# Moving the Gram parts of the fifth step and the first two output transposes to earlier places in a planned order

## The chip, the cores and the metric

The kernel runs on one core of a Trainium2 chip. The metric is device time of one execution in microseconds (us). A profile of one further execution gives, for each engine, when every instruction started and how long it took. Engines: PE is the matrix engine (TensorE; its weight loads are listed apart as PEld), DVE the vector engine, ACT the scalar engine, POOL is GpSimd, SP only issues transfers. Each engine works through its own instructions strictly in the order of the program; where one has to wait, everything behind it on that engine waits too.

## The reference, cut to what matters

Three stages follow each other. The first is a linear attention with a delta rule, token after token (4 batches, 8 heads, 768 tokens, 48 columns per head):

```python
for t in range(S):
    kt, vt, bt = (k_n[:, :, t], v[:, :, t], beta[:, :, t, None])
    y[:, :, t] = np.einsum('bhd,bhde->bhe', q[:, :, t], state)
    v_old = np.einsum('bhde,bhd->bhe', state, kt)
    state = state + bt[:, :, :, None] * np.einsum('bhd,bhe->bhde', kt, vt - v_old)
```

The second is a product layer on the 3072 rows of y: `a = x @ w1; b = x @ w2; h = a * b @ w3; x = h @ w_out` (384 columns, 1024 inside). The third is a soft mixture of experts: `logits = x @ phi`, a softmax over all tokens that makes 32 slot inputs, two layers per expert, a softmax over the slots that spreads the results back.

## The kernel before, in words

**Attention in chunks.** The 768 tokens are cut into 24 steps of 32 tokens; all 4 batches and 8 heads of a step are worked on together. Two steps make a pair (12 pairs, the tiles `kl` of keys and queries are loaded per pair, the names kl_112 to kl_115 are the first four pairs), four steps make a group (6 groups). For each step, small matmuls make its Gram parts (`g_step`, L474 on: keys times keys and keys times queries, into PSUM banks gp). Their evacuation (`g_evac`, L432 on) has three pieces: DVE masks the key part into the tile dg (L437), ACT copies a part to the buffer `praw` (L448) and four blocks to kl (L472), and POOL multiplies praw by a mask into kl (L457 or L464). From dg, a group's four steps together, DVE solves the small triangular systems (`solve_steps`; the transpose L519 starts it, then some 20 us of short dependent DVE operations, L607 ends it). A step's chain (`chain_steps`) then runs: POOL scales v (`pre`, L660), PE takes the old values (ks, L674) which DVE subtracts (L676), PE applies the solve (vp, L685), ACT copies the result into sv (L649), PE makes the outputs (yp, L695; ACT copies them to ys, L698) and, once in a pair, the new state (sacc, L705; ACT copies it to sv, L649). The last part of a step's chain, `xt`, turns the outputs ys by three PE transposes (xp, L717), which ACT rounds (L720) and DVE subtracts (L721) into the tile xT that the product layer reads.

**Product layer.** For each pair 8 products `ab` (18 matmuls each, L770) with w1 and w2; ACT and DVE multiply the halves (L774, L779). w3, w_out and phi are folded into one 1024x32 matrix, wphi.

**Weights.** All of w1, w2, w3 and w_out arrive as 64-bit floats and are converted on the chip (`to_f32`, L325 to L342): five operations, DVE L333, ACT L334, DVE L335, L337 and L339, then a product L342 on POOL (or DVE). w1 and w2 come first (tiles gx, raw_w and t_w; results wsl, with a rounding rest `lo` made by PE L358 and L359 and copied by ACT L360). Then w_out and w3 in 32 pieces of the tile `hold`: 8 of wo, then 24 of w3, each with PE transposes (wot L386, w3tw L407), an ACT copy (woT L388, w3T L409) and a PE product (wm L391, w3tw L411).

**What sets the order.** Every piece of work is put into a list with a number, its place (`when`, `spread`); the list is sorted by it, and the pieces are recorded in that order, which gives each instruction its priority. A planner then goes through the program with a model of the engines and lets each engine take the ready instruction of the highest priority, so that a piece with an earlier place can also move others. Numbers below zero are work ahead of the first product. `G1` is the place of the Gram parts of pair 2 (the fifth and sixth step, tile kl_114), `G2` that of pair 3 (kl_115); the second group's solve, solve 1 (dg, gl_1441, w_1535), needs both. PSUM buffers are handed out in recorded order too: the Gram parts of the second group use the two banks of `ab`, where a bank's next user waits until the last one is evacuated. The buffers of praw have the tag ys, of which there are two, shared with the outputs ys and with the solve's t. SP issues nearly all transfers in one queue; a reload of a kl tile waits there until the pair before is done with it.

## Time and profile before

| | |
|---|---|
| median of 3 runs | 621.5 us (618.1 to 623.37) |
| the profiled execution's own time | 618.01 us |
| its span in the profile | 616.2 us |
| PE busy | 566.3 us (92%) |
| DVE busy | 392.6 us (64%) |
| ACT busy | 282.4 us (46%) |
| POOL busy | 126.1 us (20%) |
| mean granted clock of PE | 0.933 |

Times within the profile count from the start of the span. A granted clock of 1.00 is 2.4 GHz and 0.50 is 1.2 GHz; a stretch with a number between had both. The first 98 us hold the first group's solve, the conversion of w1 and w2 and the chains of the first steps; solve 1 runs from 98 to 121 us; from there on products, chains and solves run side by side, with the conversion of wo and w3 up to about 215 us. The experts fill the last 60 us.

### The profile page before, as it was taken

To read this page: it belongs to the slowest core of one execution; us is meant where nothing else is said; L and a number is where in the kernel's file an instruction comes from. 1 tells how busy PE (TensorE), PEld (TensorE's weight loads), DVE (VectorE), ACT (ScalarE), POOL (GpSimd) and SP (SyncE) were. 2 spreads that over 40 slices of the span, in tenths; PEclk is the share of its full clock that TensorE was granted. 3 is DMA by queue.
4 is the path that set the end of the run, shared out by engine and by line. 5 is a ranking of instruction groups with operands and counts; after the bars stand their busy time and mean duration, and the time that the engine had idled before them with its cause. 6 is when DMAs were issued, how large, how long until landed. Compare 5 with 4: busy or idle time off the path is not lost.

```text
span 616.2 us, 26161 instructions
## 1 busy us (share of the span) xinstructions
PE 566.3 (92%) x11506; PEld 460.1 (75%) x11508; DVE 392.6 (64%) x1275; ACT 282.4 (46%) x709; POOL 126.1 (20%) x191
## 2 busy tenths in 40 slices
PE   4888769797989999999989999999999999999996
PEld 3455558696777878879879897988988888885364
DVE  6997786977699549832499827987981313224124
ACT  1147674455466454654535545435444354323023
POOL 0111185253464260122200103013111000000100
PEclk7678866989698999999999999999999999999997
DMA  5934881048547732401304040312425133689818
GB/s 121 287 98 149 221 223 55 3 137 254 168 131 214 202 82 68 100 17 28 90 3 101 16 101 16 111 53 80 139 87 196 53 110 99 229 274 319 333 63 278
DMA packets 36945, 81.73 MB, mean 133 GB/s; under 512 B 4352, under 2 KB 17792, under 8 KB 35584
## 3 DMA queue, kind: packets, MB, share of 16 engines
q1 hardware_dynamic: 36544, 79.54, 43.2%
q8 instruction: 90, 1.47, 1.0%
q10 hardware_dynamic: 288, 0.52, 0.4%
q14 instruction: 23, 0.19, 0.1%
HBM read 69.57 MB, written 10.49 MB: 130 GB/s over the span
## 4 chain that ended last, share of the span: by engine, by line
PE 48%; DVE 35%; POOL 5%; ACT 4%; DMA 3%; issue 3%; SPq 1%; DVEq 0%; POOLq 0%; ACTq 0%
PE ab L770 19%; DVE xl L581 6%; DVE tmp L578 6%; PE gp L492 2%; PE vp L685 2%; PE sacc L1215 2%; DVE gl L519 2%; PE gp L787 2%; PE hp L1194 2%; PE ks L674 2%; DMA hold<-wo 2%; DVE xl L556 2%; PE w3tw L407 2%; DVE gT L779 2%; PE yp L695 2%
## 5 line engine op out<-in xcount | busy, mean ns | idle before, releaser
L770 PE MATMUL ab<-xT,wsl 128*128 128x256 f32 x1728 | 243.3, 293 | 0.3 <-DVE gT L779 0.2
L770 PEld LDWEIGHTS ab<-xT,wsl 128*128 128x128 f32 x1728 | 218.6, 194 | 11.3 <-issue 5.7
L779 DVE TENSOR_TENSOR gT<-ab,bs 128x256 f32<-128x256 f32 x84 | 35.0, 420 | 85.1 <-ACT bs L774 84.4
L774 ACT COPY bs<-ab 128x256 f32<-128x256 f32 x96 | 35.6, 372 | 79.7 <-PE ab L770 76.2
L660 POOL TENSOR_TENSOR v<-v,nnT 128x384 f32<-128x384 f32 x24 | 21.0, 873 | 193.0 <-DMA v<-vt 86.7
L581 DVE TENSOR_TENSOR xl<-xl,tmp 128x84 f32<-128x84 f32 (+35 forms) x220 | 51.1, 263 | 0.8
L649 ACT COPY sv<-vp 32x384 f32<-32x384 f32 x96 | 45.2, 471 | 11.7 <-PE vp L685 10.0
L578 DVE TENSOR_TENSOR tmp<-xl 128x84 f32<-128x84 f32 (+35 forms) x220 | 47.5, 246 | 0.5
L492 PE MATMUL gp<-kl 48*32 48x128 f32 (+1 forms) x1152 | 37.7, 265 | 4.7 <-ACT kl L472 4.6
L342 POOL TENSOR_TENSOR hold<-hold 128x384 f32<-128x384 f32 (+1 forms) x32 | 31.7, 991 | 42.6 <-DVE hold L339 15.1
L472 ACT COPY kl<-gp 32x256 f32<-32x256 f32 x72 | 26.2, 364 | 22.6 <-DVE kl L457 21.7
L492 PEld LDWEIGHTS gp<-kl 48*32 48x32 f32 x1152 | 27.0, 115 | 12.5 <-ACT kl L472 6.1
L788 ACT COPY gtok<-gp 128x512 f32<-128x512 f32 x48 | 28.2, 588 | 16.4 <-PE gp L787 15.6
L787 PE MATMUL gp<-cs,gT 128*128 128x128 f32 x168 | 26.7, 277 | 2.1 <-DVE gT L779 1.8
L335 DVE SCALAR_TENSOR_TENSOR hold<-hold 128x384 int32<-128x384 int32 (+1 forms) x32 | 22.5, 702 | 8.0 <-ACT hold L334 7.5
L674 PE MATMUL ks<-sv,kl 48*32 48x48 f32 (+2 forms) x1344 | 24.4, 212 | 2.2 <-issue 1.6
L334 ACT ACTIVATE hold<-hold,cs 128x384 int32<-128x384 int32 (+1 forms) x32 | 18.9, 590 | 16.4 <-DVE hold L333 15.3
L685 PEld LDWEIGHTS vp<-v,w 32*32 32x32 f32 x1536 | 20.3, 110 | 7.3 <-issue 3.6
L685 PE MATMUL vp<-v,w 32*32 32x48 f32 x1536 | 25.1, 210 | 0.6 <-DVE w L634 0.6
L674 PEld LDWEIGHTS ks<-sv,kl 48*32 48x32 f32 (+2 forms) x1344 | 20.1, 113 | 6.9 <-issue 3.6
L695 PE MATMUL yp<-sv,kl 112*32 112x48 f32 (+2 forms) x1408 | 24.7, 209 | 0.4 <-issue 0.4
L695 PEld LDWEIGHTS yp<-sv,kl 112*32 112x32 f32 (+2 forms) x1408 | 19.5, 110 | 5.3 <-issue 2.6
(252 smaller groups left out, 965.5 us busy)
## 6 DMA issues: line engine op xcount, KB each, us to landing
hold<-w SPq DMA_DIRECT2D x16, 384.0 KB, 3.7
v<-vt SPq DMA_DIRECT2D x24, 192.0 KB, 2.9
kl<-kq SPq DMA_DIRECT2D x9, 512.0 KB, 7.4
kk<-kt SPq DMA_DIRECT2D x12, 384.0 KB, 6.2
kl<-w1e SPq DMA_DIRECT2D x6, 768.0 KB, 5.4
unitg<-w2e SPq DMA_DIRECT2D x6, 768.0 KB, 4.7
kl<-kq SPq DMA_DIRECT2D x9, 384.0 KB, 5.0
gx<-w SPq DMA_DIRECT2D x4, 768.0 KB, 5.2
```

What stands on the lines that cost most here:

```text
L342: last_m.append(E.tensor_tensor(out=w, in0=m, in1=w, op=ALU.mult))
L492: m = T.matmul(gp[trow(n, b), h - hs[0]], lhsT=t[r, k[j], kc], rhs=t[r, slots, kc], start=True, stop=True)
L578: V.tensor_tensor(out=tmp[:, 0:n, lo:hi], in0=x[:, j + 1:32, j:j + 1].to_broadcast([128, n, hi - lo]), in1=x[:, j:j + 1, lo:hi].to_broadca ...
L581: V.tensor_tensor(out=x[:, j + 1:32, lo:hi], in0=x[:, j + 1:32, lo:hi], in1=tmp[:, 0:n, lo:hi], op=ALU.add)
L649: A.copy(o, i)
L674: T.matmul(kp[o, h], lhsT=kl[r, (5, 1)[b // 2] if t2 else 3, kcol(h, b)], rhs=sv[r, b, h * D:(h + 1) * D], start=True, stop=True, tile_pos ...
L685: T.matmul(p[o, h * D:(h + 1) * D], lhsT=w[o, 8 * n4 + h, :], rhs=r[o, h, :], start=True, stop=True, tile_position=(o.start, o.start))
L695: T.matmul(p[qrow(b), h * D:(h + 1) * D], lhsT=kl[r, (6, 0)[b // 2] if t2 else (4, 2)[b // 2], kcol(h, b)], rhs=sv[r, b, h * D:(h + 1) * D ...
L770: T.matmul(o, lhsT=w[:, m, k], rhs=x[:, k], start=(n == 0), stop=(n == 8))
L774: A.copy(bs, p[:, 256:512])
L779: V.tensor_tensor(out=gt, in0=p[:, 0:256], in1=bs, op=ALU.mult)
L787: T.transpose(p[:, t * 256 + i * 128:t * 256 + (i + 1) * 128], gt[:, t * 128:(t + 1) * 128], ident)
```

## The change

Three numbers move. The Gram parts of pair 2 get the place -0.55 instead of -0.439. The last part of the chain of step 0 and of step 1, the transposes of the outputs with their rounding, is taken out of the spread and gets a place of its own, -0.6 and -0.5. In the spread they stood at -0.574 and, with the shift that the table SHIFT gives to chain1, at about -0.34. The list GAB names the steps whose Gram parts use the banks of `ab`; it names the same four as the condition `n // 4 == 1` did.

```diff
-G1 = -0.439
+G1 = -0.55
...
 HP = 7
+XE = (-0.6, -0.5)
+GAB = (4, 5, 6, 7)
...
-        p = (ab if n // 4 == 1 else at)(f"{which}{n}_{hs[0]}")
+        p = (ab if n in GAB else at)(f"{which}{n}_{hs[0]}")
...
     for n in range(NST):
         steps = chain_steps(n)
+        if n < 2:
+            when(XE[n], steps[-1], label=f"x{n}")
+            steps[-1] = lambda: None
         spread(ct(n / 2), ct(n / 2 + 0.5), steps, f"chain{n}")
```

No instruction is added or removed, apart from where the planner cuts a run of equal ones in pieces. The line numbers of the changed kernel are higher by 2 from L90 on, and by 5 from L987 on. What moves is shown at three places.

**First place: ACT during the chain of step 1.** The names: ys_949 are the outputs of step 0, vp_985 (vp_993 in the change) the solved values of step 1, praw_0, praw_4 and kl_114 the evacuation of the two halves of the fifth step's Gram parts. ACT before:

```order
L698 COPY ys_949<-yp_916 128x384
L334 ACTIVATE t_w_858<-t_w_858,cs 128x768
L354 CAST wsl_106<-t_w_819 128x768
L360 CAST wsl_106<-lo_827 128x384
L360 CAST wsl_106<-lo_831 128x384
L649 COPY sv<-vp_985 32x384 x4
L720 CAST xT_0_1022<-xp_1024 128x3x128
L354 CAST wsl_107<-t_w_841 128x768
L334 ACTIVATE hold<-hold,cs 128x384 x3
```

ACT in the change:

```order
L700 COPY ys_949<-yp_916 128x384
L450 COPY praw_0_1049<-gp_0_1031 64x128 x2
L336 ACTIVATE t_w_858<-t_w_858,cs 128x768
L474 COPY kl_114<-gp_0_1031 32x2x4x32 x4
L722 CAST xT_0_985<-xp_987 128x3x128
L450 COPY praw_4_1076<-gp_4_1058 64x128 x2
L474 COPY kl_114<-gp_4_1058 32x2x4x32
L356 CAST wsl_106<-t_w_819 128x768
L474 COPY kl_114<-gp_4_1058 32x2x4x32 x3
L362 CAST wsl_106<-lo_827 128x384
L362 CAST wsl_106<-lo_831 128x384
L651 COPY sv<-vp_993 32x384 x4
```

Twelve copies of the evacuation (two times two of praw, two times four of kl_114) and the rounding of the first transposes now stand ahead of the copies of vp. Before, they stood behind the outputs ys_1063 of step 1.

PE at the same place, before (lo are parts of the conversion of w1 and w2, xp the transposes, gp_0_1122 the sixth step's Gram parts, which come 16 rows further down):

```order
L359 MATMUL lo_827<-wsl_106,nid 128x384
L359 MATMUL lo_831<-wsl_106,nid 128x384
L685 MATMUL vp_985<-v_331,w_428 32x48 x32
L717 MATMUL xp_1024<-cs,ys_949 128x128 x3
L705 MATMUL sacc_110<-sv,kk_835 48x48
L358 MATMUL lo_849<-t_w_841,cs 128x384
L358 MATMUL lo_853<-t_w_841,cs 128x384
L705 MATMUL sacc_110<-sv,kk_835 48x48 x11
L695 MATMUL yp_1030<-sv,kl_112 32x48 x11
L359 MATMUL lo_849<-wsl_107,nid 128x384
L359 MATMUL lo_853<-wsl_107,nid 128x384
L695 MATMUL yp_1030<-sv,kl_112 32x48 x21
```

PE in the change (gp_0_1085 are the sixth step's Gram parts, gp_0_1346 the first half of the seventh's, from kl_115; yp_1126 the outputs of step 1):

```order
L494 MATMUL gp_0_1085<-kl_114 32x64 x12
L687 MATMUL vp_993<-v_331,w_428 32x48 x29
L361 MATMUL lo_827<-wsl_106,nid 128x384
L361 MATMUL lo_831<-wsl_106,nid 128x384
L687 MATMUL vp_993<-v_331,w_428 32x48 x3
L494 MATMUL gp_0_1085<-kl_114 32x64 x20
L494 MATMUL gp_0_1346<-kl_115 32x128 x10
L360 MATMUL lo_849<-t_w_841,cs 128x384
L360 MATMUL lo_853<-t_w_841,cs 128x384
L494 MATMUL gp_0_1346<-kl_115 32x128
L697 MATMUL yp_1126<-sv,kl_112 32x48
L707 MATMUL sacc_110<-sv,kk_835 48x48 x4
```

The Gram parts of the sixth step and most of the first half of the seventh's now stand inside the chain of step 1, ahead of its outputs.

**Second place: POOL ahead of solve 1.** Here hold are products of the conversion of wo, v_1474 the scaled values of step 3. POOL before:

```order
L660 TENSOR_TENSOR v_1065<-v_1065,nnT_314 128x384
L342 TENSOR_TENSOR t_w_858<-gx,t_w_858 128x768
L660 TENSOR_TENSOR v_1474<-v_1474,nnT_314 128x384
L342 TENSOR_TENSOR hold<-hold 128x384
L457 TENSOR_TENSOR kl_114<-praw_0_1086,cs 64x256
L342 TENSOR_TENSOR hold<-hold 128x384
L457 TENSOR_TENSOR kl_114<-praw_0_1086,cs 64x256
L342 TENSOR_TENSOR hold<-hold 128x384 x2
L457 TENSOR_TENSOR kl_114<-praw_4_1113,cs 64x256 x2
L464 TENSOR_TENSOR kl_114<-praw_0_1156,cs 32x8x32 x4
L342 TENSOR_TENSOR hold<-hold 128x384
L457 TENSOR_TENSOR kl_115<-praw_0_1364,cs 64x256 x2
```

POOL in the change:

```order
L662 TENSOR_TENSOR v_1161<-v_1161,nnT_314 128x384
L459 TENSOR_TENSOR kl_114<-praw_0_1049,cs 64x256 x2
L459 TENSOR_TENSOR kl_114<-praw_4_1076,cs 64x256 x2
L344 TENSOR_TENSOR t_w_858<-gx,t_w_858 128x768
L662 TENSOR_TENSOR v_1474<-v_1474,nnT_314 128x384
L466 TENSOR_TENSOR kl_114<-praw_0_1119,cs 32x8x32 x4
L344 TENSOR_TENSOR hold<-hold 128x384 x4
L459 TENSOR_TENSOR kl_115<-praw_0_1364,cs 64x256 x2
L459 TENSOR_TENSOR kl_115<-praw_4_1391,cs 64x256 x2
L466 TENSOR_TENSOR kl_115<-praw_0_1434,cs 32x8x32 x4
```

The mask products of the fifth step's Gram parts went from between the hold products to a place ahead of t_w_858, those of the sixth step from behind four hold products to ahead of them, and the fifth hold product went from ahead of the seventh step's mask products to behind solve 1's part of this queue. DVE and ACT likewise convert four pieces of wo ahead of solve 1 now, where they converted five. SP issues the reload of kl_112 behind the stores of these four products now, and issued it ahead of the first of them before.

**Third place: ACT at the end of solve 1.** Here bs and ab are the first pair's products, praw_0_1804 belongs to the tenth step's Gram parts, woT are turned pieces of wo. ACT before:

```order
L448 COPY praw_4_1761<-gp_4_1743 64x128 x2
L472 COPY kl_112<-gp_4_1743 32x2x4x32 x4
L774 COPY bs_3_1830<-ab_3_1811 128x256
L448 COPY praw_0_1804<-gp_0_1770 64x256 x2
L388 COPY woT_1866<-wot_1862 128x384
L334 ACTIVATE hold<-hold,cs 128x384
L774 COPY bs_4_2083<-ab_4_2064 128x256
L388 COPY woT_1887<-wot_1883 128x384
```

ACT in the change:

```order
L450 COPY praw_4_1761<-gp_4_1743 64x128 x2
L474 COPY kl_112<-gp_4_1743 32x2x4x32 x4
L776 COPY bs_3_1830<-ab_3_1811 128x256
L390 COPY woT_1845<-wot_1841 128x384
L450 COPY praw_0_1804<-gp_0_1770 64x256 x2
L336 ACTIVATE hold<-hold,cs 128x384
L776 COPY bs_4_2083<-ab_4_2064 128x256
L390 COPY woT_1866<-wot_1862 128x384
L336 ACTIVATE hold<-hold,cs 128x384
```

The copy of the first turned piece of wo, woT_1845, stands ahead of praw_0_1804; before it came much earlier, and the copy of the second, woT_1866, stood directly behind praw_0_1804. PE's products with these pieces (wm) moved in the same way, each to about one piece later.

## Rows read from the trace of the kernel before

**Rows 1.** Busy time by stretch: stretch, its length, busy us of PE, PEld, DVE, ACT, POOL (instructions), granted clock, DMA

```profile
69.00:84.00 15.00, 11.37 (x337) 8.32 (x329) 10.90 (x18) 12.54 (x29) 6.87 (x6) 0.96 0.95 259
98.00:123.00 25.00, 21.09 (x417) 19.10 (x409) 23.82 (x94) 9.02 (x26) 8.49 (x11) 0.89 0.03 8
123.00:216.00 93.00, 87.30 (x1709) 70.43 (x1713) 69.09 (x161) 50.29 (x121) 38.52 (x42) 0.89 0.64 183
345.00:555.00 210.00, 206.20 (x4270) 183.49 (x4269) 115.90 (x423) 94.29 (x235) 20.98 (x46) 1.00 0.37 115
```

**Rows 2.** The chain of waits, 62 to 128 us: start, length, what

```profile
66.30 10.25 DMA hold<-wo
...
91.93 0.26 ACT praw L448
...
94.04 1.08 PE gp L492 x32
...
97.63 0.43 DVE dg L437
...
98.08 1.99 DVE gl L519
...
121.36 0.42 DVE dg L437
...
122.64 0.49 ACT woT L388
```

**Rows 3.** Instructions in order of time, POOL: start, length, what [idle before, ended by]

```profile
70.68 1.85 POOL L342 TENSOR_TENSOR t_w<-gx,t_w 128x768 f32<-128x768 f32 x1 [8.80 <-DVE gx L339]
...
88.37 3.52 POOL L464 TENSOR_TENSOR kl<-praw,cs 32x256 f32<-32x256 f32 x4
```

**Rows 4.** The same of ACT, from the outputs of step 0 on

```profile
62.98 0.50 ACT L698 COPY ys<-yp 128x384 f32<-128x384 f32 x1
...
65.48 0.84 ACT L354 CAST wsl<-t_w 128x768 fp32r<-128x768 f32 x1 [0.80 <-DVE t_w L342]
68.45 0.86 ACT L360 CAST wsl<-lo 128x384 fp32r<-128x384 f32 x2 [2.14 <-PE lo L359]
69.95 1.94 ACT L649 COPY sv<-vp 32x384 f32<-32x384 f32 x4 [0.64 <-PE vp L685]
...
78.76 0.55 ACT L448 COPY praw<-gp 64x128 f32<-64x128 f32 x2
79.33 1.49 ACT L472 COPY kl<-gp 32x256 f32<-32x256 f32 x4
80.85 1.93 ACT L649 COPY sv<-sacc 48x384 f32<-48x384 f32 x4
...
86.02 0.76 ACT L448 COPY praw<-gp 64x256 f32<-64x256 f32 x2
```

**Rows 5.** The same of DVE, conversion of wo

```profile
72.84 0.36 DVE L333 TENSOR_SCALAR hold<-hold 128x384 int32<-128x384 int32 x1 [2.39 <-DMA hold<-wo]
74.56 0.36 DVE L333 TENSOR_SCALAR hold<-hold 128x384 int32<-128x384 int32 x1 [1.37 <-DMA hold<-wo]
...
84.35 1.25 DVE L339 SCALAR_TENSOR_TENSOR hold<-hold 128x384 f32<-128x384 uint32 x1
```

**Rows 6.** The two loads of kl_115: how often, issue time, first and last start; then time to landing

```profile
L236 SPq DMA_DIRECT2D kl<-kq x2: 423/454/484, 63.6 to 64.1; - x2
...
DMA to landing us min/median/max: 5.9/6.8/7.8
```

**Rows 7.** Instructions in order of time, PE

```profile
65.59 2.50 PE L358 MATMUL lo<-t_w,cs 128*128 128x384 f32 x4 [1.93 <-DVE t_w L342]
...
108.83 1.08 PE L492 MATMUL gp<-kl 48*32 48x128 f32 x32
...
123.18 0.85 PE L391 MATMUL wm<-phis,woT 128*128 128x32 f32 x6 [2.18 <-ACT woT L388]
...
150.25 0.41 PE L407 MATMUL w3tw<-cs,hold 128*128 128x128 f32 x2 [2.49 <-ACT part L415]
```

## The prediction

> **What bounds the kernel now.** I read the busy time by stretch first [rows 1]. From 345 to 555 us PE is busy 206.2 of 210 us at full clock: whatever is won or lost before that is carried to the end, for nothing there could make it up. From 123 to 216 us it is busy 87.3 of 93, with a granted clock of 0.89, and DVE 69.1. Ahead of that, from 98 to 123, DVE is busy 23.8 of 25: this is solve 1, one operation after the other. So the question is what starts solve 1, and the chain of waits answers it [rows 2]: the load of wo lands at 76.55, DVE and POOL convert the pieces, POOL works off its mask products, and ACT may only then start on the seventh step's Gram part (91.93, praw), ends with it at 94.04, PE fills the bank that this frees, DVE masks the last part at 97.63 and the transpose of solve 1 begins at 98.08. The wait is one for a buffer: POOL reads praw of the sixth step until 88.37 + 3.52 = 91.89 [rows 3], and there are two such buffers. In the order of time, ACT shows why POOL is so late [rows 4]: the fifth step's parts are evacuated from 78.76 on, in the order of ACT behind the outputs of step 1, though ACT had 0.80 + 2.14 + 0.64 = 3.58 us of waits between 64 and 70 us.

> **Part 1: the Gram parts of the fifth and sixth step.** None of PE's matmuls for the fifth step moves; its evacuation does. On ACT this is two times 0.55 and two times 1.49 [rows 4], 4.1 us, and with the first rounding (0.50, as the copy of ys) 4.6 us, put between the end of ys (63.48) and the copies of vp (69.95). The waits there take up 3.6, so chain 1 is late by at most 1.0 us; the rounding no longer stands behind those copies, which gives back 0.5. I take +0.5 for chain 1. POOL's four mask products, 0.88 each as in the four of [rows 3], 3.5 us, fall into its wait of 8.80 us before 70.68 and cost POOL nothing.

> What decides is when ACT can begin with the seventh step's part (91.93 before). Three things must be there.
> - The praw buffer. POOL's four products for the sixth step now stand ahead of the hold products, and ACT delivers their input amid the first conversions of wo, so POOL is through with them before these products; the buffer that it waited for until 91.89 is no longer the last.
> - ACT itself. The copies of the new state end at 80.85 + 1.93 = 82.78 [rows 4]. Ahead of them now come the praw copies of the sixth step (0.76) and the second rounding (0.50), behind them the short copy t, which takes under 0.5 us by the size of ys. With the 0.5 of chain 1 that is 85.0 at the latest.
> - DVE's mask of the same part, which stands behind the four conversions and the second subtraction of xT. The conversions ended at 84.35 + 1.25 = 85.60 [rows 5]. They can't start sooner, because the loads of wo set their start (DVE waited 2.39 and 1.37 us for them), and I let them end as before. The subtraction has 384 columns where the mask of [rows 2] took 0.43 for 256, so 0.65 by estimate, and the mask at most 0.43: 86.7.

> DVE is the latest, so ACT begins at 86.7 instead of 91.93: **-5.2 us** for the start of solve 1. Bounds: with DVE out of the way ACT's 85.0 gives -6.9; and 0, if chain 1 becomes the last (second rival).

> The sixth step's Gram matmuls and ten rows of the seventh's now stand in PE's queue inside chain 1. The seventh's wait for kl_115: its second load goes out at 64.1 and lands 7.8 us later at most, at 71.9 [rows 6], and outputs and state of step 1 stand behind it. PE is idle for 15 - 11.4 = 3.6 us between 69 and 84 [rows 1], and the wait from 69 is 2.9, so I cost it at nothing; without that cover it costs 2.9.

> [...] DVE converts w1 and w2 between 64 and 70 us without a pause while POOL waits; four POOL products of 0.88 now run beside it. A product of 384 columns took DVE 1.25 us at 84.35 beside POOL. If DVE waited each time for the whole product, its conversions would be late by 4 x 0.88 = 3.5 us. Behind them DVE waits 2.39 + 1.37 = 3.8 us for the loads of wo [rows 5], so the four conversions of wo still start by the loads, and the sum stays. [...]

> **Part 2: the two transposes.** Each is three matmuls, an ACT rounding and a DVE subtraction. The first goes into a gap of PE: it waited 1.93 us before 65.59 [rows 7]. The second stands ahead of the last eight rows of the state's matmuls and waits there for ACT's copy of ys: 0.50, within the sum for ACT above only as the rounding. I give it 0.5 more at ACT (85.5), still ahead of DVE's 86.7. No product waits for either: the first product starts behind the Gram parts in PE's queue, which now come sooner by the same 5.2.

> **Part 3: what follows by itself.** (a) At the end of solve 1 PE stood idle for 2.18 us until 123.18 [rows 7], waiting for woT, which ACT took behind a praw copy, which waited for DVE's mask at 121.36 [rows 2]. In the change the woT needed there stands ahead of that praw copy. The next thing PE wants is a bank that DVE frees just after its mask, so a part comes back: between 0 and -2.2 I take **-1.5**, since PE has 46 matmuls for the next step to do meanwhile. (b) Four pieces of wo are converted ahead of solve 1, not five, so 28 remain instead of 27. At 93 / 27 = 3.4 us per piece that is the most it can cost; nothing is the least, because each piece's consumers on PE stand about one piece later too. PE is the fuller engine there, 87.3 against 69.1, so I take 0. (c) SP's reload of kl_112 waits behind the stores of the four products: DVE's 85.6, a POOL product of 384 columns, up to 1.3 by the widths of [rows 3], about 1.1 for issuing, and 7.8 to land make 95.8. Its first reader, a Gram part, ran at 108.83 [rows 7] and comes 5.2 sooner, at 103.6. The cover is 7.8 us; beyond it each us would delay PE.

> **Sum.** -5.2 - 1.5 = -6.7 us. Against the profiled execution's own 618.0 that is 611.3. This execution is 3.5 below the median of the runs shown, 621.5; so I predict 621.5 - 6.7 = **614.8 us**.

> **Rivals.**
> 1. More than that. After 123 us the clock of 0.89 means 0.22 x 93 = 20 us at 1.2 GHz, which cost about half of that, 10 us [rows 1]. Stalls of PE such as the 2.49 us at 150.25, which waited for the w3 conversion, fall into this stretch. If the shift to one piece later also removes that stall and half of the slow time, it is another -2.5 - 5: about 607. For it: consumers stand later relative to conversions. Against: other stalls can arise as well. 0.15.
> 2. **Chain 1 becomes the last, and the kernel slower.** After its wait of 1.93 us PE took 2.50 us for four matmuls [rows 7], and in the change it waits twice more in this chain, for kl_115 and for ys. If it runs at 1.2 GHz from 69 to 84, its 11.4 us of work there [rows 1] at most doubles; with the 2.9 of the load of kl_115 chain 1 would be 14.3 late, less the 3.6 of waits already there, 10.7. The cover is from 85.5 to 91.93, 6.4 us: from there on solve 1 starts later than before. 10.7 - 6.4 = +4.3 for solve 1, and if the piece of (b) then costs its 3.4 too, 621.5 + 7.7 = 629. Against: the clock of this stretch was 0.96 before, and the stretch has more work now. 0.11.
> 3. The gain is given back by the conversions: -5.2 + 3.4, and the stall of 2.18 is replaced by one for a bank. 619.7. For it: from 123 us on the chain of conversions ended several of PE's waits. 0.19.
> 4. It doesn't do what it says: the list GAB changes no bank, and if the seventh step's part is still the last by the buffers, solve 1 starts as before. 621.5. Against: the buffer's reader on POOL has clearly moved ahead of the products. 0.05.

> The forecast itself gets 0.50, with 611 to 618 around it (-3.5 to -10 by the bounds of parts 1 and 3).

> **Chances.** A measurement of this kernel can tell about 1%, 6.2 us, from no change; faster by that is below 615.3. The forecast lies just beyond it, so it gives 0.29 of its 0.50 to faster and 0.21 to the same; rival 1 is faster; rivals 3 and 4 are the same; of rival 2, 0.09 is slower and 0.02 the same. Faster 0.44, same 0.47, slower 0.09. The range reaches from 606, rival 1 with a little more, to 623, which takes in rivals 3 and 4 and leaves out rival 2.

> **What would show it.** Right: the evacuation of kl_114 on ACT at 64 to 70 us; the transpose of solve 1 at 92 to 94 us; the chain of waits coming to it through DVE's conversions, no longer through POOL's L464 (L466 in the change) and praw; no wait of PE for woT at its end; the distance kept at 345 us. Wrong: solve 1 after 96 us with the copies of the state on ACT after 88; PE at 1.2 GHz from 69 to 84; a new wait of PE for converted pieces between 115 and 215; a Gram part that waits for kl_112.

## The result, and the profile after

The changed kernel took **627.75 us** in the median of 4 runs (626.33 to 631.56), the kernel before 619.8 in the runs beside it (617.99 to 623.37): ratio **1.0128**, 95% interval 1.0080 to 1.0176. It is slower by about 8 us, against a forecast of 614.8 and a range of 606 to 623. The profiled execution took 626.33 us, its span is 624.5 us, 8.3 more than the 616.2 of before, and the clock was 0.947 against 0.933.

What the change does to ACT, POOL and DVE happened as forecast. ACT, in order of time (start, length, what, and in brackets the idle time before and what ended it):

```profile
63.36 0.50 ACT L700 COPY ys<-yp 128x384 f32<-128x384 f32 x1
63.73 0.55 ACT L450 COPY praw<-gp 64x128 f32<-64x128 f32 x2
64.31 0.94 ACT L336 ACTIVATE t_w<-t_w,cs 128x768 int32<-128x768 int32 x1
65.27 1.49 ACT L474 COPY kl<-gp 32x256 f32<-32x256 f32 x4
...
68.84 1.12 ACT L474 COPY kl<-gp 32x256 f32<-32x256 f32 x3
```

The fifth step's parts are evacuated from 63.73 on, not from 78.76 as in [rows 4]. POOL takes their products at once and is not on the way to solve 1 any more:

```profile
64.07 2.87 POOL L459 TENSOR_TENSOR kl<-praw,cs 64x256 f32<-64x256 f32 x2 [1.98 <-ACT praw L450]
67.49 2.12 POOL L459 TENSOR_TENSOR kl<-praw,cs 64x256 f32<-64x256 f32 x2 [0.55 <-ACT praw L450]
```

The chain of waits to solve 1, the lines that answer to [rows 2] (start, length, what):

```profile
66.80 9.53 DMA hold<-wo
...
85.53 1.25 DVE hold L341
...
86.79 0.48 DVE xT L723
...
89.73 2.47 issue
...
96.07 3.79 issue
...
100.57 0.43 DVE dg L439
...
101.02 1.99 DVE gl L521
```

The chain now comes through DVE's conversions, as forecast. They end at 85.53 + 1.25 = 86.78 (forecast 85.6), the second subtraction ends at 87.27, DVE's mask of the same part follows, and ACT takes the seventh step's part at 87.54 (forecast 86.7, before 91.93):

```profile
87.54 0.55 ACT L450 COPY praw<-gp 64x128 f32<-64x128 f32 x2 [2.48 <-DVE dg L439]
```

But the solve starts at **101.02**, not near 93, and later than the 98.08 of before. Between the two stand 2.47 and 3.79 us called "issue": time in which TensorE waited for nothing that the profile shows. TensorE in the same stretch:

```profile
87.40 1.05 PE L626 MATMUL j<-t,sums 32*32 32x16 f32 x64 [1.66 <-DVE xT L723]
88.38 1.34 PE L676 MATMUL ks<-sv,kl 48*32 48x48 f32 x56
92.20 0.38 PE L676 MATMUL ks<-sv,kl 48*32 48x48 f32 x8 [2.47 <-issue]
92.37 1.69 PE L494 MATMUL gp<-kl 48*32 48x128 f32 x40
93.99 1.50 PE L687 MATMUL vp<-v,w 32*32 32x48 f32 x64
95.42 0.65 PE L494 MATMUL gp<-kl 48*32 48x64 f32 x15
99.86 0.65 PE L494 MATMUL gp<-kl 48*32 48x64 f32 x15 [3.79 <-issue]
```

The reader is to see that both stops fall inside a run of equal matmuls: 56 of 64, then 8; 15 of 30, then 15. The matmuls behind a stop read the same tiles and fill the same bank as those ahead of it. And 8 + 40 + 64 + 15 = 127 matmuls lie from one stop to the next. Busy time by stretch, columns as in [rows 1], of the changed kernel:

```profile
84.00:88.00 4.00, 2.34 (x144) 2.07 (x135) 3.42 (x6) 1.49 (x5) 2.54 (x4) 0.87 0.89 266
88.00:92.00 4.00, 1.73 (x91) 1.50 (x83) 0.35 (x1) 1.54 (x5) 1.33 (x2) 0.50 1.02 328
92.00:96.00 4.00, 3.80 (x127) 3.29 (x128) 0.75 (x2) 2.33 (x7) 1.44 (x2) 0.50 1.03 214
96.00:100.00 4.00, 0.21 (x11) 0.14 (x11) 0.00 (x0) 1.52 (x4) 0.00 (x0) 0.50 0.54 139
```

and of the kernel before:

```profile
88.00:92.00 4.00, 3.00 (x132) 2.37 (x125) 2.74 (x5) 0.34 (x2) 3.62 (x6) 0.50 0.59 211
92.00:96.00 4.00, 2.92 (x100) 2.30 (x103) 0.76 (x2) 3.34 (x11) 3.48 (x5) 0.50 0.49 141
96.00:100.00 4.00, 4.00 (x131) 3.67 (x124) 2.34 (x2) 3.42 (x9) 1.26 (x3) 0.50 0.20 64
```

From 96 to 100 hardly anything but ACT works in the changed kernel. The last number but one is the transfers' share: 1.02 and 1.03 in the stretch of the first stop and in the next, 0.54 in that of the second; before it fell from 0.59 to 0.49 and 0.20. The loads and stores of wo are issued from 83 to 88 us (before 81 to 87). In the kernel before most of the dense matmuls came behind them, from 92 on; now they come beside them, and so does the reload of kl_112 and kk (issued at 88.80, before at 75.04).

A third stop lies further ahead, at the seventh step's first Gram matmuls, where the prediction had put a wait of up to 2.9 us for kl_115:

```profile
74.74 0.81 PE L494 MATMUL gp<-kl 48*32 48x128 f32 x18 [2.23 <-issue]
```

The second load of kl_115 had landed at 72.3, so it is no wait for that. Nor is it on the way to solve 1, which leads through the load of wo and DVE. e13 and e15, which share this order of the first steps, have it too (2.71 and 4.04 us), the kernel before has none there.

Where the 8.3 us of the span went, by the starts of the solves (solve 2 and 3 at 215.60 and 299.75 before, 219.55 and 307.25 after): 2.9 ahead of solve 1, 1.0 from solve 1 to 2, 3.5 from 2 to 3, and 0.8 from there to the end.

### The profile page after: what moved, and what is told of

The parts are those of the page before. It is cut to its first block, busy times and chain, and to the rows that moved or that the text cites. A ratio compares the mean times of both kernels' runs of the same rounds, so it can differ in the third digit from the quotient of the medians.

```text
span 624.5 us, 26160 instructions
## 1 busy us (share of the span) xinstructions
PE 569.4 (91%) x11508; PEld 463.7 (74%) x11508; DVE 393.7 (63%) x1275; ACT 282.5 (45%) x709; POOL 130.2 (21%) x191
## 3 DMA queue, kind: packets, MB, share of 16 engines
q8 instruction: 90, 1.47, 1.0%
## 4 chain that ended last, share of the span: by engine, by line
PE 49%; DVE 33%; DMA 6%; POOL 4%; issue 4%; ACT 3%; SPq 1%; DVEq 0%; POOLq 0%; ACTq 0%
PE ab L772 20%; DVE tmp L580 5%; DVE xl L583 5%; DMA hold<-w 3%; PE gp L789 2%; PE vp L687 2%; PE sacc L1220 2%; PE gp L494 2%; PE ks L676 2%; DVE gl L521 2%; PE hp L1199 2%; PE yp L697 2%; PE sacc L707 2%; DVE xl L558 2%; DMA hold<-wo 2%
## 5 line engine op out<-in xcount | busy, mean ns | idle before, releaser
L772 PE MATMUL ab<-xT,wsl 128*128 128x256 f32 x1728 | 246.4, 295 | 4.0 <-DVE gT L781 2.0
L772 PEld LDWEIGHTS ab<-xT,wsl 128*128 128x128 f32 x1728 | 221.0, 196 | 15.3 <-issue 5.8
L651 ACT COPY sv<-vp 32x384 f32<-32x384 f32 x96 | 45.2, 471 | 11.5 <-PE vp L687 9.8
L583 DVE TENSOR_TENSOR xl<-xl,tmp 128x84 f32<-128x84 f32 (+35 forms) x220 | 48.1, 249 | 0.7
L344 POOL TENSOR_TENSOR hold<-hold 128x384 f32<-128x384 f32 (+1 forms) x32 | 33.3, 1041 | 48.2 <-DVE hold L341 24.7
L697 PE MATMUL yp<-sv,kl 128*32 128x48 f32 (+2 forms) x1408 | 25.2, 208 | 0.0
```

The source lines that it names most:

```text
L344: last_m.append(E.tensor_tensor(out=w, in0=m, in1=w, op=ALU.mult))
L583: V.tensor_tensor(out=x[:, j + 1:32, lo:hi], in0=x[:, j + 1:32, lo:hi], in1=tmp[:, 0:n, lo:hi], op=ALU.add)
L651: A.copy(o, i)
L697: T.matmul(p[qrow(b), h * D:(h + 1) * D], lhsT=kl[r, (6, 0)[b // 2] if t2 else (4, 2)[b // 2], kcol(h, b)], rhs=sv[r, b, h * D:(h + 1) * D ...
L772: T.matmul(o, lhsT=w[:, m, k], rhs=x[:, k], start=(n == 0), stop=(n == 8))
```

## The experiments

Three theories at first. **T1**: transfers that run beside TensorE's small matmuls keep its instructions from coming (the page of the kernel before lists a queue called "instruction", 90 packets, 1.47 MB, 1.0% of the same 16 engines of which the data's queue takes 43.2%). It began as "the late reload of kl_112" and was widened to all transfers. **T2**: a dense run of small matmuls outruns the coming of instructions by itself. **T3**: the fifth wo piece, which the changed kernel converts behind solve 1, is what the rest lacks. Later **T5**: from the first to the second solve TensorE is the bound, and the share of low clock sets the length.

All numbers in one table. "Ratio" is to the kernel before in the same comparison. "To solve 1" counts from the end of TensorE's wait for t_w (65.59 before, [rows 7]; 66 to 69 in other runs), so that a later start of the stretch does not count. "Stops" are TensorE's waits of over 1 us without a visible releaser, from 84 us to solve 1. The last three columns are the stretches from solve 1 to 2, with its granted clock, and from 2 to 3. All but the ratio are from one profile each, and executions of one kernel differ by several us (the kernel before took 615.7 to 624.8 in the runs beside e8), so a difference of 1 or 2 us between two profiles can be chance. The rest behind solve 3, not in the table, is 316.5 us before, 317.3 in the changed kernel and 316.4 to 321.2 in the others; the longest is that of e14, whose ratio is 1.

| kernel | ratio (95%) | to solve 1 | stops | 1 to 2 | clock | 2 to 3 |
|---|---|---|---|---|---|---|
| before | 1 | 32.5 | 1.6 | 117.5 | 0.89 | 84.2 |
| changed | 1.0128 (1.0080 to 1.0176) | 34.6 | 6.3 | 118.5 | 0.90 | 87.7 |
| e1 transposes alone | 1.0163 (1.0097 to 1.0229) | 36.8 | 5.2 | 121.0 | 0.90 | 83.7 |
| e2 Gram parts alone | 1.0135 (1.0078 to 1.0192) | 33.2 | 6.2 | 123.7 | 0.87 | 83.8 |
| e3 changed, reload late | 1.0127 (1.0068 to 1.0187) | 32.1 | 2.9 | 121.3 | 0.88 | 87.7 |
| e4 before, reload late | 1.0036 (1.0001 to 1.0071) | 36.1 | 3.4 | 117.0 | 0.90 | 83.8 |
| e5 before, fifth piece later | 1.0100 (1.0062 to 1.0139) | 32.0 | 0 | 122.3 | 0.86 | 83.8 |
| e6 before, loads held | 0.9992 (0.9955 to 1.0030) | 32.9 | 1.8 | 115.5 | 0.91 | 84.1 |
| e7 changed, transfers held | 1.0099 (1.0066 to 1.0132) | 32.5 | 5.5 | 119.8 | 0.88 | 87.6 |
| e8 the same, held longer | 1.0085 (1.0053 to 1.0116) | 30.3 | 1.4 | 115.1 | 0.94 | 86.9 |
| e9 before, held longer | 1.0023 (0.9998 to 1.0049) | 32.6 | 0 | 117.1 | 0.88 | 84.2 |
| e10 changed, fifth piece sooner | 1.0174 (1.0128 to 1.0221) | 37.4 | 6.2 | 124.1 | 0.86 | 81.7 |
| e11 e10, transfers held | 1.0083 (1.0050 to 1.0117) | 35.0 | 2.0 | 123.8 | 0.89 | 81.1 |
| e12 e2, loads held | 1.0159 (1.0120 to 1.0199) | 31.5 | 2.9 | 125.6 | 0.85 | 83.7 |
| e13 changed, a piece left out | 1.0149 (1.0112 to 1.0185) | 39.4 | 7.8 | 123.7 | 0.86 | 82.3 |
| e14 before, a piece left out | 1.0000 (0.9977 to 1.0023) | 33.0 | 1.6 | 116.3 | 0.89 | 83.7 |
| e15 e13, transfers held | 1.0055 (1.0026 to 1.0084) | 30.2 | 2.5 | 122.8 | 0.85 | 82.5 |
| e16 before, a wait filled | 1.0032 (1.0005 to 1.0060) | 33.0 | 0 | 115.9 | 0.91 | 87.2 |

### The two halves, and the reload

e1 is the changed kernel with the Gram parts back in their place, e2 the kernel before with the Gram parts alone moved:

```diff
 e1, in the changed kernel        e2, in the kernel before
-G1 = -0.55                       -G1 = -0.439
+G1 = -0.439                      +G1 = -0.55
```

> The transposes alone; the Gram parts of the fifth step keep their old place. The plan evacuates them late, as before, puts the reload of kl_112 between and behind the stores of the first wo pieces (as the change does) and keeps five pieces of wo ahead of solve 1. Theory T1 (the late reload shares the DMA engines with PE's instruction fetches and so stops PE ahead of solve 1): PE waits without a visible releaser of 2 us and more between 85 and 98 us, solve 1 at 99 to 102 us, 620 to 626 us in all. Theory T2 (the instructions come at their own pace, and only a dense run of small matmuls outruns it): solve 1 at 97 to 99 us, 618 to 621. Theory T3 (the missing fifth piece of wo costs the rest later): no extra loss after solve 1, since five are converted ahead.

> The Gram parts alone; the transposes stay in the spread. The plan evacuates the fifth step's parts early, as the change does, but issues the reload of kl_112 early, as before, and keeps five pieces of wo ahead of solve 1. T1: no traffic beside the fetches from 88 to 96 us, so solve 1 at 92 to 95 us, some 4 us sooner than before, and with T3 nothing lost later: 613 to 617 us. T2: the small matmuls are as dense as in the change, so PE waits for instructions as there and solve 1 begins at 99 to 101: 619 to 623.

Each half alone costs as much as both. In e2 the reload of kl_112 stays early, and yet TensorE stops for 2.19 and 3.97 us ahead of solve 1: the reload alone is not the reason, and the first form of T1 fell. e3 holds the reload in the changed kernel, e4 delays it in the kernel before:

```diff
 e3
+    def late_load(p):
+        gate[:] = last_g
+        load(p)
+        load_kk(1)
+        gate.clear()
...
-            when(t, lambda p=p: load(p))
+            when(t, (lambda p=p: late_load(p)) if p == 4 else (lambda p=p: load(p)))
 e4: the same with gate[:] = [g_at[6, 0]], the matmuls of the seventh step's first half
```

> The change, with one thing altered: the reload of kl_112 and of the next kk waits until the last Gram matmul of kl_115, so that it starts about when solve 1 does. The order on PE, DVE, ACT and POOL is that of the change. T1: PE's waits of 2.5 and 3.8 us ahead of solve 1 shrink to under 1.5 together, solve 1 at 95 to 97 us instead of 101.0, the time 4 to 6 us below the change: 621 to 623.5; with T3 the later loss of 5 us stays. T2: both waits stay, solve 1 at 100 to 101, 626 to 628 us.

> The kernel before, with one thing altered: the reload of kl_112 and of the next kk waits for the first half of the seventh step's Gram matmuls and is issued at about 88 us, behind the stores of four pieces of wo, as in the change. The order on PE, DVE, ACT and POOL is that of before. T1: PE waits of 2 to 6 us without a visible releaser appear between 88 and 98 us (1.57 before), solve 1 at 100 to 103 us instead of 98.1, the time 622 to 626 us. T2: solve 1 stays at 98 to 98.5 and the time at that of before, 618 to 621.

e3: the stops shrink from 6.3 to 2.9 us (1.70 at the ks, 1.19 at an earlier Gram part; the second one is gone), but the time does not move (1.0127). e4: the reload beside the dense stretch makes one stop of 3.35 us, solve 1 starts 3.6 us later by the profile, and the time is 1.0036 (1.0001 to 1.0071). So the reload can make such a stop; it is one transfer among several.

### All transfers away from the dense stretch

Here the order on TensorE, VectorE, ScalarE and GpSimd stays exactly that of the kernel compared with; only SP's transfers move.

```diff
 e6 (first piece held: 5) and e7 (4, with the edit of e3)
+LATE = [f"wo{g}" for g in range(5, 8)]
...
-            gate[:] = [last_v[LW]]
+            gate[:] = [g_at[6, 0]] if name in LATE else [last_v[LW]]
 e8 (as e7) and e9 (as e6): g_at[7, 0], the last Gram matmuls ahead of solve 1
```

> The kernel before, with the loads of the sixth to eighth wo pieces (384 KB each) held until the last Gram matmuls ahead of solve 1; the order on TensorE, VectorE, ScalarE and GpSimd is unchanged. T1, widened after the first runs (any transfers, not the reload alone, keep TensorE's instructions from coming while it runs small matmuls): the wait of 1.57 us at 92.57 without a visible releaser is gone, DMA share under 0.5 from 84 to 96, solve 1 starts 1 to 3 us sooner counted from TensorE's first wo transposes' stretch, and the time is 0 to 3 us less, 617 to 620 us, if the pieces that come late (near 98 to 103, needed from 123) are covered. T2 (instructions come at a pace of their own that a dense run outruns): the wait stays as it is, and solve 1 does not move.

> The changed kernel, with the loads of the fifth to eighth wo pieces and the reload of kl_112 and kk held until the last Gram matmuls ahead of solve 1; the order on the four compute engines is that of the changed kernel. T1 (widened): from 84 to 98 only the four stores of 192 KB move, the two waits without a visible releaser of 2.47 and 3.79 us ahead of solve 1 shrink to under 1 us together, and solve 1 starts 4 to 6 us sooner than in the changed kernel, at 95 to 97 us by a profile whose first conversions are at the same place; the time 4 to 6 us less than the changed kernel's, 622 to 624. T2: the two waits stay, 5 us or more together, solve 1 at 100 to 101 us, and the time 627 to 629.

e7 missed its aim, and that told more than a hit: the seventh step's first half was done at 91.89, the loads went out, and the stops followed. Busy time by stretch in e7:

```profile
88.00:92.00 4.00, 3.95 (x219) 3.23 (x223) 3.24 (x7) 2.90 (x9) 2.64 (x3) 1.00 0.29 102
92.00:96.00 4.00, 1.75 (x116) 1.47 (x107) 0.84 (x3) 1.19 (x5) 0.88 (x2) 1.00 0.77 202
96.00:100.00 4.00, 1.42 (x71) 1.06 (x59) 0.00 (x0) 3.78 (x10) 1.44 (x2) 0.52 0.85 293
```

With the transfers' share at 0.29, TensorE went through 219 matmuls in 4 us without a stop, more than in any stretch of the changed kernel; with 0.77 and 0.85 it stood for 2.25 and 3.26 us. **As the whole account T2 falls here**: this dense row made no such stop. Something of it is left, as e11 will show. e6's loads, too, went out at 88.56 already; the time did not change.

> The changed kernel as in e7_after_quiet, but with the loads of the fifth to eighth wo pieces held behind the very last Gram matmul ahead of solve 1; in e7 they were let go at 91.89 already, and its two waits without a visible releaser (2.25 ending 94.66, 3.26 ending 100.68) stand behind that, while 80 to 92 with a DMA share under 0.3 had none at 219 matmuls in 4 us. T1 (any transfers keep TensorE's instructions from coming): no such wait over 1 us from 84 to the start of solve 1, which comes 4 to 6 us sooner than the changed kernel's counted from the end of the last conversion ahead of it (before 98.1, after 101.0): near 97 to 98 where the first transposes stand 2 us late as in e7, else 95 to 96. T2: the two waits stay.

> The kernel before, with the loads of the sixth to eighth wo pieces behind the very last Gram matmul ahead of solve 1; order of the four compute engines unchanged. T1: the wait without a visible releaser at 92.57 (1.57 us; 1.84 in e6, whose loads went out at 88.56) is gone, solve 1 starts 1.5 to 3 us sooner, and, as the later stretches do not change (117.5 and 84.1 us), the time is 1.5 to 3 us less than before, 617 to 619. T2: no change.

TensorE in e8, the lines that answer to those of the changed kernel:

```profile
88.43 1.05 PE L626 MATMUL j<-t,sums 32*32 32x16 f32 x64 [2.15 <-DVE xT L723]
89.41 1.34 PE L676 MATMUL ks<-sv,kl 48*32 48x48 f32 x56
92.13 0.39 PE L676 MATMUL ks<-sv,kl 48*32 48x48 f32 x8 [1.37 <-issue]
92.30 1.69 PE L494 MATMUL gp<-kl 48*32 48x128 f32 x40
93.92 1.50 PE L687 MATMUL vp<-v,w 32*32 32x48 f32 x64
95.35 1.25 PE L494 MATMUL gp<-kl 48*32 48x64 f32 x30
```

Matmul for matmul the same order. The first stop is there at the same matmul with 1.37 instead of 2.47 us (only stores move, a share of 0.29), the second is gone (share 0.02), and solve 1 starts at 97.11, 4.3 us sooner counted from the wait for t_w. The time is 1.0085; its interval overlaps that of the changed kernel, and the profiled execution is the fastest of ten (619.21, median 625.18). Two further pairs of one order, below, are clear of each other. e9: the stop of 1.57 is gone as T1 said, but solve 1 does not move. In its place TensorE waits 2.17 us at 96.48 for ACT's kl: in the kernel before, POOL and ACT set the start of solve 1 [rows 2], and the stop was beside that way.

### The fifth piece of wo

e5 sends the piece behind solve 1 in the kernel before. e10 brings it ahead of solve 1 in the changed kernel, and e11 is e10 with the transfers held as in e8 (first piece held: 5). e12 is e2 with the loads held as in e9.

```diff
 e5
+    def behind1(f): # tc.issue_after(ends[1].ins) around f
...
-    spread(TW0, TW1, [behind_w12(f, 7) for f in wo_steps() + w3_steps()], "w3")
+    spread(TW0, TW1, [behind_w12(f, 7) if i != 4 else behind1(f) for i, f in enumerate(wo_steps() + w3_steps())], "w3")
 e10
+    ws = wo_steps() + w3_steps()
+    when(-0.0155, *[behind_w12(f, 7) for f in ws[:5]], label="wo")
+    spread(TW0, TW1, [lambda: None] * 5 + [behind1(f) for f in ws[5:]], "w3")
```

> The kernel before, with the fifth of the eight wo pieces converted behind solve 1 instead of ahead of it; every other instruction in its order. T3 (the piece that the changed kernel no longer converts ahead of solve 1 is what it lacks later): the second solve starts 2 to 4 us later after the first than the 117.5 us of before, or the stretch from the second to the third solve grows from 84.15 us towards the 87.7 us of the changed kernel; 3 to 6 us more in all, 623 to 627 us. T3 wrong: both stretches stay within 1 us, 619 to 622 us, and the growth of that stretch in the changed kernel is from the transposes' new place.

> The changed kernel, with the fifth wo piece converted ahead of solve 1 again, in the time in which VectorE waits for TensorE there (between its masks of the last two Gram parts). T3 (the piece behind solve 1 costs 4 to 5 us later, as in e5_before_piece5, where it cost 4.8 between the first and the second solve): the stretch from the second to the third solve falls from 87.7 to 84 us, that from the first to the second stays under 119, solve 1 starts within 2 us of the changed kernel's, and the time is 3 to 5 us less than its 627.75: 622 to 625. If T3 is wrong, 626 to 629. (T1 expects the two waits of 2.47 and 3.79 us to stay.)

> The kernel of e10_after_piece5 (fifth wo piece ahead of solve 1 again), with the loads of the sixth to eighth pieces and the reload of kl_112 and kk held behind the last Gram matmuls, as in e8_after_quieter; order of the four compute engines that of e10. In e10 the waits without a visible releaser (3.62 ending 94.90, 2.62 ending 104.25) left TensorE at a mean granted clock of 0.59 from 104 to 123. T1: those two waits shrink to under 1.5 us together, solve 1 starts 4 to 6 us sooner counted from TensorE's stop at the fourth conversion, and with it the clock there and the stretch to the second solve come back from 124.1 to 117 to 119 us. T3 then shows without that cover: the stretch from the second to the third solve stays at 82 to 84 us (after 87.7), and the time is 3 to 5 us under the 625.2 of e8: 620 to 622. If the piece is not the cause, 625 to 627.

> The kernel of e2_g1_only (the fifth step's Gram parts sooner, the transposes where they were, reload of kl_112 early), with the loads of the sixth to eighth wo pieces held behind the last Gram matmuls; order of the compute engines that of e2. T1: its waits without a visible releaser of 2.19 (ending 88.37) and 3.97 us (ending 96.34) shrink to under 1.5 us together, solve 1 starts about 4 us sooner counted from TensorE's stop at the fourth conversion (e2: 33.2 us after it), and the time falls from 629.0 to 622 to 625, to the lower end or under it if the low clock between the first and the second solve (123.7 us there) was of those waits. T2: 628 to 630.

e5 costs 1.0100, as T3 said, but from solve 1 to 2 (122.3), not from 2 to 3. e10: the stretch from 2 to 3 falls from 87.7 to 81.7, but the time does not fall (1.0174, its interval overlaps that of the changed kernel). e11 has the order of e10 on all four engines, and only its transfers moved: **1.0174 (1.0128 to 1.0221) became 1.0083 (1.0050 to 1.0117)**, the stops ahead of solve 1 went from 6.2 to 2.0. That is T1 in the time. The second stop is gone, the first is still 1.98 us long:

```profile
94.87 0.29 PE L676 MATMUL ks<-sv,kl 48*32 48x48 f32 x8 [1.98 <-issue]
```

```profile
88.00:92.00 4.00, 4.00 (x213) 3.47 (x207) 1.39 (x3) 3.44 (x10) 1.54 (x3) 1.00 0.32 116
92.00:96.00 4.00, 2.02 (x107) 1.49 (x99) 1.06 (x4) 1.28 (x4) 1.04 (x2) 1.00 0.01 4
```

It falls into a stretch in which next to no transfer ran (share 0.01), behind one of 213 matmuls at full clock. So a dense row had a stop of 1.98 us here with next to no transfer beside it, and that much is left of T2; with the transfers, in e10, the first stop was longer (3.62 us) and the second, of 2.62 us, was there. And e11 is no faster than e8, so the piece ahead of solve 1 gains nothing by this edit. e12 is a miss for T1's forecast of the time: the stops fell from 6.2 to 2.9 and solve 1 came 1.7 sooner, and the stretch to solve 2, with the lowest clock of the table (0.85, as in e15), took it back. Six pairs with moved Gram parts have one order, and transfers moved away in one of the two: the changed kernel with e3, e7 and e8, e2 with e12, e10 with e11, e13 with e15. The stops are shorter in all six, the time is clear of the counterpart's in the last two.

e13 takes the piece away altogether, e14 is the control, e15 is e13 with the transfers held as in e8:

```diff
             V.tensor_copy(mwp[:, g, :], p[:, 0:32])
+            if g == 3:
+                V.tensor_copy(mwp[:, 4, :], p[:, 0:32])
+                SP.dma_start(out=wod[:, 4, :], in_=w)
...
-        return [lambda g=g: cv(g) for g in range(8)]
+        return [(lambda: None) if g == 4 else (lambda g=g: cv(g)) for g in range(8)]
```

> The changed kernel with the fifth of the eight wo pieces left out (its 384 KB load, its conversion and its matmuls; the fourth piece's result stands for it in the product and in the store), so that three pieces are left behind solve 1, as many as in the kernel before. T3 (what the changed kernel loses behind solve 1 is the one piece more that is converted there): from the first solve to the third 201 to 203 us as before (201.65; changed 206.2), the logits' first matmuls 8 to 9 us after the start of the second solve (before 8.85, changed 10.74), time 622 to 624. If the loss behind solve 1 is of the new order and not of the piece: 205 us or more, and the time 626 or more.

> Control: the kernel before with the same piece left out, so that two are left behind solve 1. Where the stretch behind solve 1 is bounded by the pieces in any case, one fewer gives 3 to 5 us here too (616 to 618), and e13 has to be read against that; where before has room for its three pieces, 619 to 621.

> Both suspected costs taken away together: the changed kernel with the fifth wo piece left out as in e13, and with the loads of the sixth to eighth and the reload of kl_112 and kk behind the last Gram matmuls as in e8. T1 and T3 together: the waits without a visible releaser ahead of solve 1 under 2 us, solve 1 starts 2 us sooner than before counted from TensorE's stop at the fourth conversion, 200 to 203 us to the third solve, time 617 to 620, at or under the kernel before. If either is wrong, over 622.

e13, with less work than the changed kernel, is no faster: 1.0149. Its stretches ahead of solve 1 tell why:

```profile
88.00:92.00 4.00, 2.78 (x119) 2.21 (x114) 0.96 (x3) 3.46 (x10) 1.86 (x3) 1.00 0.83 253
92.00:96.00 4.00, 2.90 (x128) 2.29 (x127) 0.35 (x1) 0.78 (x3) 0.59 (x1) 0.54 1.08 313
96.00:100.00 4.00, 0.00 (x0) 0.00 (x0) 0.00 (x0) 0.00 (x0) 0.00 (x0) 0.50 0.96 174
```

For 4 us no engine does anything while the transfers are at 0.96; TensorE's stop is 6.13 us long, the longest of all. e15 has the same order with those transfers held: **1.0149 (1.0112 to 1.0185) became 1.0055 (1.0026 to 1.0084)**, the second pair. As for T3: without the piece, 82.3 and 82.5 us from solve 2 to 3 instead of 87.7, but 123.7 and 122.8 from 1 to 2 instead of 118.5, so the sum is 206.0 and 205.2 against 206.2. In the changed order the 3.5 us between solve 2 and 3 go with the piece, **but as an account of the loss T3 falls**, since what is won there is lost one stretch sooner. Why it is lost there isn't shown. The control e14 stays at 1.0000: the kernel before has room for its pieces.

### What sets the stretch from solve 1 to 2

The stretches from solve 1 to 2 (columns as in [rows 1]) of before, the changed kernel, e8 and e12:

```profile
98.08:215.60 117.52, 107.91 (x2116) 89.22 (x2109) 92.46 (x253) 58.98 (x144) 47.01 (x52) 0.89 0.51 146
```

```profile
101.02:219.55 118.53, 107.07 (x2108) 90.31 (x2100) 94.39 (x257) 58.85 (x143) 49.90 (x53) 0.90 0.49 144
```

```profile
97.11:212.17 115.06, 103.62 (x2108) 87.44 (x2100) 93.95 (x256) 58.88 (x144) 49.97 (x53) 0.94 0.59 173
```

```profile
99.77:225.34 125.57, 114.81 (x2120) 94.68 (x2115) 93.02 (x254) 59.27 (x146) 46.64 (x52) 0.85 0.51 150
```

Take from each length TensorE's idle time (length less busy) and what the clock is short of 1, times the length: 117.5 - 9.6 - 12.9 = 95.0; 118.5 - 11.5 - 11.9 = 95.2; 115.1 - 11.4 - 6.9 = 96.7; 125.6 - 10.8 - 18.8 = 96.0. Over all the kernels of the table it is 93 to 99, so what this sum leaves unexplained is itself up to 5 us between two kernels. In these four it differs by less than 2, and idle time and the time at a clock of 0.50 make up the rest; the two that share an order (changed and e8) differ by 5 us of clock. e16 tried to change that:

```diff
+    FILL = 24
...
+    def fill(o, n):
+        for _ in range(n):
+            T.matmul(o, lhsT=zw, rhs=zw, start=True, stop=True)
...
+            fill(p[:, 0:128], FILL if (f, j0) == (0, 3) else 0)
```

> The kernel before, with 24 matmuls of 128x128 (bf16, on constants, into columns that nobody reads any more) on TensorE behind the products of the second w3 piece, where it stood idle for 2.49 us until 150.25 and ran at a granted clock of 0.50 from 152 to 165 after that. T5 (between the first and the second solve TensorE is the bound, and kernels differ there by its low-clock stretches: length less idle time less the share lost to the clock is 93 to 97 us in every kernel run so far): the granted clock of that stretch rises from 0.89 to 0.93 or more, its length falls from 117.5 by about the clock share given back, 4 to 6 us, and the time is 614 to 617. If the low clock there is not what sets the length (the conversions of w3 are), the clock rises and the length stays within 1 us: 620 to 621. If the idle time isn't what lets the clock fall, neither changes.

```profile
148.38 1.51 PE L159 MATMUL w3tw<-cs 128*128 128x128 bf16 x24
151.30 0.41 PE L414 MATMUL w3tw<-cs,hold 128*128 128x128 f32 x2 [1.41 <-ACT part L423]
```

The 24 matmuls took 1.51 us, and a wait of 1.41 was left; the granted clock fell to 0.50 from about 153 to 166 as before. The stretch was 1.6 us shorter (115.9, clock 0.91), the next one 3 us longer, and the planner's order changed behind the new matmuls (the logits' first matmuls come 13.27 us after the start of solve 2, before 8.85). It failed to keep the clock up, so T5 as a cause is not shown; what stands is the sum above.

## Why the prediction was wrong

**The start of solve 1, -5.2: this is the step that failed.** Its first half, how soon ACT can take the seventh step's part, was right in its mechanism and 0.8 us short: 87.54, forecast 86.7, so that -5.2 became -4.4. Here DVE's conversions of wo were the mis-sized term. They were let end as before, at 85.60, and ended at 86.78; POOL's products of the sixth step ran beside them now (from 77.83, 3.66 us), and the prediction had asked only whether these keep POOL's buffer. For the conversions of w1 and w2 the cover was needed: DVE waited only 1.04 and 0.35 us for the loads of wo where it had waited 2.39 and 1.37 [rows 5], so 2.4 of the 3.8 us were used up. The prediction put 3.5 us on DVE's conversions beside the four products of the fifth step. Four of DVE's operations there took 1.48, 1.08, 1.17 and 1.48 us, before 0.95, 0.56, 0.95 and 0.95, which is 1.8 us more, and the products 2.87 + 2.12 = 5.0 us, forecast 3.5. So both sides took longer, the four products too (3.6 us before); that DVE pays for the products in full, 3.5 us, no run shows.

```profile
74.44 0.95 DVE L335 TENSOR_SCALAR hold<-hold 128x384 int32<-128x384 int32 x1 [1.04 <-DMA hold<-wo]
...
76.36 0.36 DVE L335 TENSOR_SCALAR hold<-hold 128x384 int32<-128x384 int32 x1 [0.35 <-DMA hold<-wo]
```

Its second half let solve 1 follow ACT at the distance of before, 98.08 - 91.93 = 6.15 us, which gave 92.85. But behind DVE there now stood a row of 262 small matmuls in TensorE's own queue (64 j, 64 ks, 40 gp, 64 vp, 30 gp). From 87.40 to 101.02 they took 13.6 us: 7.4 without the stops, 6.3 in stops. Worked out again from ACT's 87.54: -4.39, and 13.48 us from there to solve 1 where 6.15 were forecast, of which 6.26 are stops and 1.07 the row; in all +2.94, as measured. The prediction named TensorE as not the last and did not ask what transfers would run beside it. That the transfers make the stops long is shown by e8, e11 and e15 (1.4, 2.0 and 2.5 us in all, against 6.3, 6.2 and 7.8), each of one order with its counterpart; 1.4 to 2.5 us of the first one stay there.

**The reload of kl_112, 0 (c).** No Gram part waited for it, as forecast; the cover held. But the step priced only its reader. Moved from 75.04 to 88.80 it takes its share of the 1.02 that TensorE's instructions had to get through. It is not the only one: e3 held it alone and the time stayed.

**TensorE's wait at the end of solve 1, -1.5 (a).** It stayed: 2.28 us, now for another thing.

```profile
128.47 1.46 PE L393 MATMUL wm<-phis,woT 128*128 128x32 f32 x6 [2.28 <-DVE mwp L394]
```

**One piece fewer ahead of solve 1, 0 of at most 3.4 (b).** From solve 1 to 3 the changed kernel lost 1.0 + 3.5 = 4.5 us. That the piece costs them is not shown: without it (e13) the two stretches together are as long. What goes with the 3.5 is the place of the logits. In the four kernels of the changed order (changed, e3, e7, e8) their first matmuls come 10.7 us after the start of solve 2, and the stretch to solve 3 is 86.9 to 87.7 us; before they came after 8.85 us (84.2), in e13 after 6.71 (82.3), in e16 after 13.27 (87.2). TensorE in the changed kernel there:

```profile
230.29 1.07 PE L796 MATMUL lp<-gx,wphi 128*32 128x256 f32 x16
...
235.79 0.50 PE L772 MATMUL ab<-xT,wsl 128*128 128x256 f32 x2 [1.81 <-DVE gT L781]
...
236.58 3.32 PE L772 MATMUL ab<-xT,wsl 128*128 128x256 f32 x16
```

The last products of w3 come behind solve 2, the logits with them, then TensorE waits 1.81 us for gT and runs at a clock of 0.50 for some matmuls (mean granted clock 0.65 from 236 to 240). The forecast took the lower end with the reason that consumers stand later too; from solve 2 on it did not hold.

**The rest.** The distance beyond solve 3 was kept, as forecast (317.25 against 316.45 us). Rival 2 gave the right sign and nearly the size, 629, by a way that did not happen: chain 1 was not late (ACT's copies of the state ended at 84.91, forecast 85.0 to 85.5), and the granted clock from 69 to 84 was 0.97. The case that was missing is a wait that stands in no list of waits, because nothing in the program releases it.

**What stays open.** With the stops cut to 1.4 to 2.5 us (e8, e11, e15), 3 to 5 us over the kernel before remain, more than half of the loss in two of the three. In e11 and e15 the stretch from solve 1 to 2 is 6.3 and 5.2 us longer than before, at a clock of 0.89, as before, and of 0.85. In e8 the stretch from 2 to 3 is 2.7 longer, but the profiled execution is 6 us shorter than the median, so where the median's 5 us lie it can't tell. What decides which waits there are followed by a stretch at a clock of 0.50 no run here shows, and why the early part (the wait for t_w ends at 65.6 to 69.4) differs between runs was not looked into. No version beat the kernel before: e6 with 0.9992 is level with it.

## What to carry to other kernels

When work moves sooner, follow it on the engine that does it, up to the operation that counts, and lay the transfers of that stretch beside it: a gain on one engine can move a dense row of small instructions into the time when the queues are full (here 262 matmuls, with the transfers' share at 1.02). The sign of that here was a wait without a releaser in the middle of a run of equal matmuls (2.47 and 3.79 us); where one stands, hold the transfers back without changing the order of the engines, and see whether the wait shrinks; whether the time follows is another question, to be asked of the pair of times. And a step's "cover" has to be named for the resource it uses (here the transfers), not for its reader alone.

## What the runs showed of the hardware

TensorE's runs of small matmuls stopped for up to 6.13 us without a releaser where the transfers' share was 0.5 to 1.08; where it was 0.29 to 0.47 they went on at 219 matmuls in 4 us (e7) or stopped for 1.37 (e8) and 2.53 us (e15), and where it was 0.01 one still stopped for 1.98 us (e11). The queue view shows one packet of a queue called "instruction" around each of the two stops of the changed kernel, first 88 to 92.3, then 96 to 100 us (queue, packets, MB, share of 16 engines):

```profile
q8 instruction: 1, 0.02, 1.6%
```

```profile
q8 instruction: 1, 0.02, 1.8%
```

The packets' own times agree with it. Each of the four waits of over 1 us without a releaser between 60 us and solve 1, in the kernel before and the changed one, ends 1.36 to 1.64 us after such a packet has ended:

| kernel | wait, us | packet | wait ends | next packet starts | transfers' share up to there |
|---|---|---|---|---|---|
| before | 1.57 | 90.12 to 91.01 | 92.57 | 93.77 (1.20 later) | 0.05 |
| changed | 2.23 | 72.26 to 73.38 | 74.74 | 75.99 (1.25) | 0.68 |
| changed | 2.47 | 89.44 to 90.56 | 92.20 | 97.31 (5.11) | 0.98 |
| changed | 3.79 | 97.31 to 98.49 | 99.86 | 100.96 (1.10) | 0.07 |

The one packet that came late, at a share of 0.98, is the one that the second stop waits for by this reading; in e8, where the share was 0.02, it started about 1.2 us after the first stop.

Most of the 90 packets cost no such wait: only three of over 1 us without a releaser lie in the whole changed kernel, the longest of 3.79 us (6.13 in e13). With the transfers held, e11 and e15 took 5.6 and 5.8 us less than e10 and e13 (the differences of their ratios, times 620), and their stops were 4.3 and 5.3 us shorter.

The granted clock of TensorE is 0.50 or 1.00 at every moment of the two traces, and a number between is a mean. In the kernel before, 12 of the products ab took 2.93 us at 0.50 (from 160.29) and 18 of them 2.41 us at 1.00 (from 385.77). No view gives the clock in GHz; the prediction's 1.2 GHz is the clock of 0.50, where two of these products in a row, 256 columns each, start 213 ns apart (median of 39 pairs), which is 1.2 columns per ns. The matmuls of L358, 384 columns each, start 640 ns apart there at the least and 321 ns at 1.00, which makes it 2.4 columns per ns at 1.00 by estimate.
